# Remainders on GpSimd, accumulation moved ahead of a step's side work, and one operand made later, in a fused attention and mixture-of-experts kernel

## The chip, the cores and the metric

The kernel runs on one core of a Trainium2 chip. Times are device microseconds (us) of one execution. The kernel before was timed three times: 1437.53 us in the median, from 1435.39 to 1437.68. A further execution was taken with the hardware profiler; it lasted 1436.41 us, and the span of its instructions is 1434.6 us. The program's instructions are issued in order on five engines: TensorE (PE in the profile; its weight loads are PEld), VectorE (DVE), ScalarE (ACT), GpSimd (POOL) and the DMA-issuing queue of SyncE (SP).

## The reference

The attention part compresses 576 keys and values of each head to 32 memory slots with a softmax of phi, attends to these slots, and gives x; four experts, weighted by the given probabilities, follow.

```python
a = softmax(phi over seq)                       # 8 batches, 8 heads, 576 x 32
k_m = einsum('bhsm,bhsd->bhmd', a, k)           # 32 x 64 a head
v_m = einsum('bhsm,bhsd->bhmd', a, v)
attn = softmax(q @ k_m.T / sqrt(64))            # 576 x 32 a head
x = (attn @ v_m) as 4608 x 512
out = sum over e of p[:, e] * (relu(x @ w1[e]) @ w2[e])   # 512 -> 1024 -> 512, 4 experts
```

The inputs are fp32 and so is the result.

## The kernel before, in words

**Precision by two parts.** TensorE multiplies in fp32r, so an operand is kept as two tiles: its rounded part, made by a ScalarE copy, and its remainder, which is the source minus the rounded part. The helper `split` (lines 141 to 143) does that for weights: `nc.scalar.copy`, then `eng.tensor_sub` on the engine that it is given. A product is three matmuls (high by high, high by remainder, remainder by high).

**The main loop.** x is never formed. For each pair of batches k (4 pairs) and each expert e, v_m is multiplied into w1 once (the tiles `vw`), and the attention weights `AT` are multiplied by that. One pair and expert take 32 steps, so there are 512 steps in all; step s of an expert works on one of 8 blocks j of 128 hidden units, for one of four groups of rows. In a step, `first(s + 2)` makes six matmuls into a PSUM tile `p1` (lines 553 to 555), ScalarE takes the relu (line 565), and VectorE makes the remainder (line 567). `second(s)` multiplies the hidden block of two steps earlier by w2 into two PSUM tiles `p2`, three where the rows that straddle two batches (`hm`, `mid`) come along (lines 583 to 585). There are four `p2` tiles. After the eighth block, `accumulate` (lines 603 and 605, on VectorE) multiplies them by the probabilities, adds them to `acc` in SBUF and so frees them. The group with three tiles (steps 16 to 23 of an expert) starts with two free tiles; its third is one of the two that the group before has just filled, so the first matmul on `hm` at its first step waits for the first `accumulate` instruction.

**Side work.** A table `plan` assigns everything else to steps: loading and splitting the next expert's w1 and w2 (`units_w1`, `units_w2`, one split a step), the products v by w1 (`vw_mm`, line 453 to 455, into a PSUM tile `pv`) and their split (`vw_out`, lines 473 and 474: ScalarE, VectorE, ScalarE, VectorE for the two batches), or, for the pairs that go "by four" batches, `four` (lines 506 to 509) with the operand `vs` that holds v of four batches, written by `write_vs` (lines 367 to 370) from v and its rounded part `vh`. Attention of batches 2 to 7 is spread over steps too: the softmax of phi (lines 192 to 209), its transposes (`tpa`, `tpb`), the splits of k and v (`kv_split`, lines 266 and 267, two a step), of their last 64 rows (`tail_split`, lines 252 and 253), `kv_mm` (line 278) two steps after `kv_split`, `kv_pick` (lines 311 and 312) and the scores. The PSUM tiles `p1`, `pv`, `x`, `kvp`, `tpa`, `sc` and the like share one ring of four buffers (tag `pm`), so a new one waits until the one four allocations before it has been read.

**What sets the order.** The start of the program and everything from step 36 (`FREE`) on is issued in the order in which it is written. Between them, steps 0 to 35 are ordered by the scheduling layer. Within a step the code ran `run_plan(s)` (the side work), `accumulate()`, `first(s + 2)`, `second(s)`. Sources arrive through four staging buffers by DMAs that SyncE issues three sources ahead; a buffer is free again when both parts of both its splits have been made.

Of the kernel before, what the change touches and what calls it, by code (L numbers as in the profile page):

```python
# [91 lines left out]
def body(ctx: ExitStack, tc: tile.TileContext, qm, qt, kv, kvt, phi, prob, w1, w1d, w2, out):  # L92
# [60 lines left out]
                split_w1(raw, fh, 2 * g + i, nc.vector)  # L153
        return ("w1", e, fh, g), emit

    def split_w2(k, e, j, raw):
        t = wp.tile([P, 2, DM], F32R, name="w2", tag="w2", bufs=NJ + 1)
        split(t, raw[:, j % 2, :], nc.vector)
        w2t[k, e, j] = t

    def units_w1(e, fh, g):
        kept = []
        def load(raw):
            kept.append(raw)
            split_w1(raw, fh, 2 * g, nc.vector)
        return (("w1", e, fh, g), load), lambda: split_w1(kept[0], fh, 2 * g + 1, nc.vector)

    def unit_w2(k, e, j2):
        def emit(raw):
# [4 lines left out]
    def units_w2(k, e, j2):  # L174
        kept = []
        def load(raw):
            kept.append(raw)
            split_w2(k, e, 2 * j2, raw)
        return (("w2", e, j2), load), lambda: split_w2(k, e, 2 * j2 + 1, kept[0])


    st = {}
# [72 lines left out]
    def unit_tail(b):  # L255
        def emit(raw):
            for h in range(2):
                tail_split(b, raw, h, nc.gpsimd if b == 1 else nc.vector)
        return ("kvt", b), emit

    def kv_split(b, hp, raw, c2, eng):
# [39 lines left out]
    def kv_pick(b, g):  # L301
        if g == 0:
            st["v", b] = att.tile([P, NP, M], F32, name="v", tag="v", bufs=2)
        for w in range(2):
            for i in range(2):
                r, m = slice(64 * i, 64 * i + 64), slice(M * i, M * i + M)
                lo = slice(2 * M + M * i, 2 * M + M * i + M)
                a = slice(2 * g, 2 * g + 2)
                dst = st["v", b][r, a] if w else kT[b % 4][r, a, m]
                src = st["kvp", b, g][r, :, w]  # L310
                (nc.vector.tensor_copy if i else nc.scalar.copy)(dst, src[:, :, m])
                nc.vector.tensor_add(dst, dst, src[:, :, lo])

    def unit_kv(b, hp):
# [16 lines left out]
    def v_hi(b, gs=slice(0, 2)):  # L331

        if ("vh", b) not in st:
            st["vh", b] = att.tile([P, NP, M], F32R, name="vh", tag="vh")
        split = lambda t: t.rearrange("p (g a) m -> p g a m", g=2)
        v, vh = split(st["v", b]), split(st["vh", b])
        if gs is not None:
            nc.scalar.copy(vh[:, gs], v[:, gs])
        return v, vh
# [154 lines left out]

    def four_split(raw, i):
        w = wp.tile([P, 2, 512], F32R, name="w1", tag="w1", bufs=4)
        split(w, raw[:, i, :], nc.vector)
        return w

    def four(n, e, fh, h, w):  # L500
# [114 lines left out]
    def att_units(b):  # L615
        u = [lambda g=g: (phi_turn(b, g), phi_turn_out(b, g)) for g in range(2)]
        u += [lambda: (phi_turn_tail(b), phi_turn_tail_out(b)), unit_tail(b)]
        u += [unit_kv(b, hp) for hp in range(NP)]
        def write():
            v_hi(b)  # L620
            if b < 4:
                write_vt(b)
            write_vs(b)
        u += [write]
        u += [unit_scores(b, t0) for t0 in (0, 2, 4)]
        u += [lambda t0=t0: (transposes(b, t0), transposes_out(b, t0)) for t0 in (0, 2, 4)]
        return u
# [8 lines left out]
    rest += [lambda hp=hp: vw_unit(0, 0, 1, hp, (0,), ("pm", 4)) for hp in range(NP)]  # L636
    for s, u in zip(REST_0, rest):
        at(s, u)
    at(4, lambda: (v_hi(0), write_vs(0)))

    at(UNITS_1[0], lambda: phi_chain(1))
    for i, u in enumerate(att_units(1)):
# [6 lines left out]
    def attention(b, s, scores, turns):  # L649
# [11 lines left out]
        for hp in range(NP):  # L661
            def load(raw, hp=hp):
                for c2 in range(2):
                    kv_split(b, hp, raw, c2, nc.vector)
            def multiply(hp=hp):
                for c2 in range(2):
                    kv_mm(b, hp, c2)
# [177 lines left out]

    def steps(a, b):
        for s in range(a, b):
            run_plan(s)
            accumulate()
            first(s + AHEAD)  # L850
            second(s)

# [44 lines left out]
```

## Time and profile before

| | before |
|---|---|
| median of 3 runs | 1437.53 us |
| profiled execution, its span | 1436.41 us, 1434.6 us |
| TensorE matmuls busy | 1399.7 us, 7748 instructions |
| VectorE busy | 815.8 us, 1877 instructions |
| ScalarE busy | 562.7 us, 1496 instructions |
| GpSimd busy | 29.1 us, 31 instructions |
| mean granted TensorE clock | 0.996 |

Busy time of TensorE is the union of matmuls whose ends are modelled, so matmuls overlap in it; time in which it is not busy is time in which it had nothing that could start. In the rows of groups, a line of the kernel, an engine and an operation are followed by out<-in names with their shapes and the number of instructions, then busy time in us and the mean of one in ns, then the idle time just before them and what ended it. In the table by windows, each row gives a stretch (us from the span's start), its length, the busy time of each engine with the number of instructions that it had there, the granted clock as a fraction, the DMA share and GB/s. In the list of waits, a row gives the waiting group, the group waited for, the total in us, how often, and the longest. In the timeline, a row gives start and length in us, engine, line, operation; square brackets hold idle time before it and what ended that.

### The profile page before, as it was taken

To read this page: it belongs to the slowest core of one execution; us is meant where nothing else is said; L and a number is where in the kernel's file an instruction comes from. 1 tells how busy PE (TensorE), PEld (TensorE's weight loads), DVE (VectorE), ACT (ScalarE), POOL (GpSimd) and SP (SyncE) were. 2 spreads that over 40 slices of the span, in tenths; PEclk is the share of its full clock that TensorE was granted. 3 is DMA by queue.
4 is the path that set the end of the run, shared out by engine and by line. 5 is a ranking of instruction groups with operands and counts; after the bars stand their busy time and mean duration, and the time that the engine had idled before them with its cause. 6 is when DMAs were issued, how large, how long until landed. Compare 5 with 4: busy or idle time off the path is not lost.

```text
span 1434.6 us, 21439 instructions
## 1 busy us (share of the span) xinstructions
PE 1399.7 (98%) x7748; PEld 1217.1 (85%) x7748; DVE 815.8 (57%) x1877; ACT 562.7 (39%) x1496; POOL 29.1 (2%) x31
## 2 busy tenths in 40 slices
PE   8899999999999989999999999999999999999998
PEld 7788878888888868878888888888888888888887
DVE  7885666756656576675564556646553434242432
ACT  6655445533344453453343443534332222222221
POOL 4300000000000000000000000000000000000000
PEclk9999999999999999999999999999999999999999
DMA  6532322575233243233568677686751633332201
GB/s 218 191 106 88 106 62 94 195 253 164 78 99 110 68 123 100 63 119 108 147 230 264 216 265 210 230 241 211 251 158 45 184 74 103 74 103 74 59 30 37
DMA packets 62840, 199.13 MB, mean 139 GB/s; under 512 B 10384, under 2 KB 11536, under 8 KB 62736
## 3 DMA queue, kind: packets, MB, share of 16 engines
q1 hardware_dynamic: 62736, 197.77, 44.1%
q8 instruction: 62, 1.02, 0.3%
q14 instruction: 42, 0.34, 0.1%
HBM read 146.35 MB, written 51.38 MB: 138 GB/s over the span
## 4 chain that ended last, share of the span: by engine, by line
PE 88%; DVE 6%; ACT 3%; DMA 2%; issue 1%; ACTq 0%; DVEq 0%
PE p L585 17%; PE p L583 17%; PE p L584 17%; PE p L553 9%; PE p L555 9%; PE p L554 9%; PE pv L506 2%; PE sc L383 2%; PE x L278 2%; DVE vw L474 1%; DVE w L143 1%; ACT vw L473 1%; DMA vwd<-vst 1%; PE tp L433 1%; ACT w L142 1%
## 5 line engine op out<-in xcount | busy, mean ns | idle before, releaser
L567 DVE SCALAR_TENSOR_TENSOR h<-p,h 128x256 fp32r<-128x256 f32 x512 | 214.7, 420 | 334.8 <-ACT h L565 221.3
L585 PE MATMUL p<-w,h 128*128 128x512 f32 x1024 | 402.5, 393 | 1.0 <-DVE nm L195 1.0
L583 PE MATMUL p<-w,h 128*128 128x512 f32 x1024 | 401.6, 392 | 0.0
L584 PE MATMUL p<-w,h 128*128 128x512 f32 x1024 | 400.9, 392 | 0.0
L565 ACT ACTIVATE h<-p 128x256 fp32r<-128x256 f32 x512 | 196.6, 384 | 481.5 <-PE p L555 463.1
L553 PE MATMUL p<-AT,vw 128*128 128x256 f32 (+1 forms) x1024 | 308.7, 301 | 10.5 <-DVE vw L474 5.2
L554 PE MATMUL p<-AT,vw 128*128 128x256 f32 (+1 forms) x1024 | 302.5, 295 | 0.7 <-DVE AT L445 0.7
L555 PE MATMUL p<-AT,vw 128*128 128x256 f32 (+1 forms) x1024 | 303.1, 296 | 0.1
L585 PEld LDWEIGHTS p<-w,h 128*128 128x128 f32 x1024 | 192.1, 188 | 44.4 <-DVE nm L195 1.5
L553 PEld LDWEIGHTS p<-AT,vw 128*128 128x128 f32 x1024 | 193.3, 189 | 32.7 <-issue 5.8
L583 PEld LDWEIGHTS p<-w,h 128*128 128x128 f32 x1024 | 192.7, 188 | 22.4 <-ACT h L565 0.3
L584 PEld LDWEIGHTS p<-w,h 128*128 128x128 f32 x1024 | 192.4, 188 | 22.2
L554 PEld LDWEIGHTS p<-AT,vw 128*128 128x128 f32 x1024 | 193.3, 189 | 20.4 <-DVE AT L445 1.2
L555 PEld LDWEIGHTS p<-AT,vw 128*128 128x128 f32 x1024 | 193.0, 189 | 0.5 <-issue 0.2
L143 DVE TENSOR_TENSOR w<-stage,w 128x512 fp32r<-128x512 f32 x259 | 179.0, 693 | 11.2 <-ACT w L142 4.9
L142 ACT CAST w<-stage 128x512 fp32r<-128x512 f32 x262 | 161.0, 617 | 8.2 <-DMA stage<-in_w 6.0
L567 DVE SCALAR_TENSOR_TENSOR hm<-p,hm 128x64 fp32r<-128x64 f32 x256 | 55.6, 217 | 119.4 <-ACT h L565 119.1
L565 ACT ACTIVATE hm<-p 128x64 fp32r<-128x64 f32 x256 | 56.9, 222 | 159.1 <-PE p L555 159.1
L509 DVE TENSOR_TENSOR vst<-pv,vst 128x512 fp32r<-128x512 f32 x80 | 55.3, 691 | 95.5 <-ACT vst L508 95.5
L508 ACT CAST vst<-pv 128x512 fp32r<-128x512 f32 x80 | 47.0, 587 | 125.0 <-PE pv L506 125.0
L474 DVE TENSOR_TENSOR vw<-pv,vw 64x512 fp32r<-64x512 f32 x94 | 64.4, 687 | 25.6 <-ACT vw L473 24.5
L473 ACT CAST vw<-pv 64x512 fp32r<-64x512 f32 x94 | 54.3, 581 | 43.7 <-DVE vw L474 34.1
(96 smaller groups left out, 1121.2 us busy)
## 6 DMA issues: line engine op xcount, KB each, us to landing
stage<-in_w SPq DMA_DIRECT2D x92, 512.0 KB, 4.0
vwd<-vst SPq DMA_DIRECT2D x80, 512.0 KB, 3.3
vw<-vwd SPq DMA_DIRECT2D x320, 128.0 KB, 4.0
stage<-in_w1d SPq DMA_DIRECT2D x40, 512.0 KB, 4.3
stage<-in_kv SPq DMA_DIRECT2D x32, 512.0 KB, 4.0
stage<-in_qm SPq DMA_DIRECT2D x16, 512.0 KB, 4.5
out<-acc SPq DMA_DIRECT2D x32, 256.0 KB, 2.1
ph<-in_phi SPq DMA_DIRECT2D x16, 288.0 KB, 4.2
```

The costliest lines, as they stand in the source:

```text
L142: nc.scalar.copy(dst[:, 0, :], raw)
L143: eng.tensor_sub(dst[:, 1, :], raw, dst[:, 0, :].bitcast(F32))
L473: nc.scalar.copy(t[r, 0, :], ps[r])
L474: nc.vector.tensor_sub(t[r, 1, :], ps[r], t[r, 0, :].bitcast(F32))
L553: nc.tensor.matmul(ps, w[:, 0, f], at_t[:, g, 0, c], start=g == 0, stop=False)
L554: nc.tensor.matmul(ps, w[:, 0, f], at_t[:, g, 1, c], start=False, stop=False)
L555: nc.tensor.matmul(ps, w[:, 1, f], at_t[:, g, 0, c], start=False, stop=g == 1)
L565: nc.scalar.activation(t[:, 0, to], ps[:, at_], AF.Relu)
L567: nc.vector.scalar_tensor_tensor(t[:, 1, to], ps[:, at_], 0.0, t[:, 0, to].bitcast(F32), ALU.max, ALU.subtract)
L583: nc.tensor.matmul(po[t], x[:, 0, :], w[:, 0, :], start=j == 0, stop=False)
L584: nc.tensor.matmul(po[t], x[:, 0, :], w[:, 1, :], start=False, stop=False)
L585: nc.tensor.matmul(po[t], x[:, 1, :], w[:, 0, :], start=False, stop=j == NJ - 1)
```

## The change

Five things change. The remainder of w1, w2 (in `units_w1`, `units_w2` and `four_split`) and of k and v (in `kv_split` of batches 2 to 7 and in `tail_split`) goes from VectorE to GpSimd; the rounded part stays on ScalarE. The splits that steps 0 to 35 make by `unit_w1` and `unit_w2` stay on VectorE. In `kv_pick` of batches 1 to 7 the second of each pair of copies goes from VectorE to ScalarE. `accumulate()` stands ahead of `run_plan(s)` in a step. `write_vs` of batches 0 and 1 is done at steps 20 and 21 and no longer at step 4 and in batch 1's units, and `vh` has two buffers so that it can wait that long.

```diff
-    def split_w2(k, e, j, raw):
+    def split_w2(k, e, j, raw, eng=nc.vector):
...
-        split(t, raw[:, j % 2, :], nc.vector)
+        split(t, raw[:, j % 2, :], eng)
...
-            split_w1(raw, fh, 2 * g, nc.vector)
-        return (("w1", e, fh, g), load), lambda: split_w1(kept[0], fh, 2 * g + 1, nc.vector)
+            split_w1(raw, fh, 2 * g, nc.gpsimd)
+        return (("w1", e, fh, g), load), lambda: split_w1(kept[0], fh, 2 * g + 1, nc.gpsimd)
...
-            split_w2(k, e, 2 * j2, raw)
-        return (("w2", e, j2), load), lambda: split_w2(k, e, 2 * j2 + 1, kept[0])
+            split_w2(k, e, 2 * j2, raw, nc.gpsimd)
+        return (("w2", e, j2), load), lambda: split_w2(k, e, 2 * j2 + 1, kept[0], nc.gpsimd)
...
-                tail_split(b, raw, h, nc.gpsimd if b == 1 else nc.vector)
+                tail_split(b, raw, h, nc.gpsimd)
...
-                (nc.vector.tensor_copy if i else nc.scalar.copy)(dst, src[:, :, m])
+                (nc.vector.tensor_copy if i and b == 0 else nc.scalar.copy)(dst, src[:, :, m])
...
-            st["vh", b] = att.tile([P, NP, M], F32R, name="vh", tag="vh")
+            st["vh", b] = att.tile([P, NP, M], F32R, name="vh", tag="vh", bufs=2)
...
-        split(w, raw[:, i, :], nc.vector)
+        split(w, raw[:, i, :], nc.gpsimd)
...
-        def write():
-            v_hi(b)
-            if b < 4:
-                write_vt(b)
-            write_vs(b)
-        u += [write]
+        u += [lambda: write_vt(b)]
...
-    at(4, lambda: (v_hi(0), write_vs(0)))
+    for b in range(2):
+        at(20 + b, lambda b=b: (v_hi(b), write_vs(b)))
...
-                    kv_split(b, hp, raw, c2, nc.vector)
+                    kv_split(b, hp, raw, c2, nc.gpsimd)
...
-            run_plan(s)
             accumulate()
+            run_plan(s)
             first(s + AHEAD)
             second(s)
```

Counted over the program, 224 remainders of weights (line 143), 48 of k and v (line 267) and 12 of the last rows (line 253) leave VectorE for GpSimd, and 28 small copies (line 311) leave VectorE for ScalarE.

Around step 48, VectorE's rows before. `kT` and `v` are the sums of `kv_pick`, `vt` is batch 2's v as an operand (step 48's side work), `acc` the accumulation of the group that step 47 ended:

```order
L567 SCALAR_TENSOR_TENSOR hm<-p_2069,hm 128x64
L567 SCALAR_TENSOR_TENSOR h<-p_2069,h 128x256
L143 TENSOR_TENSOR w_2089<-stage,w_2089 128x512
L354 CAST vt_82<-vh 64x2x32
...
L207 RECIPROCAL zs<-zs 128x1
L208 TENSOR_SCALAR ph<-ph,zs 128x576
L209 COPY ph<-ph 128x64
L605 SCALAR_TENSOR_TENSOR acc<-p_1879,pt,acc 128x512
L605 SCALAR_TENSOR_TENSOR acc<-p_1883,pt,acc 128x512
L567 SCALAR_TENSOR_TENSOR hm<-p_2108,hm 128x64
```

and the same place of the change:

```order
L567 SCALAR_TENSOR_TENSOR hm<-p_2069,hm 128x64
L567 SCALAR_TENSOR_TENSOR h<-p_2069,h 128x256
L605 SCALAR_TENSOR_TENSOR acc<-p_1879,pt,acc 128x512
L605 SCALAR_TENSOR_TENSOR acc<-p_1883,pt,acc 128x512
L354 CAST vt_82<-vh 64x2x32
```

The two accumulations stand right behind step 49's remainder of the hidden block; thirteen instructions that stood ahead of them (a weight's remainder, eight on `vt`, four on phi) now follow or are gone.

Around steps 157 to 159, VectorE's rows before, where w2's remainder stands ahead of `vw_out` in each step:

```order
L567 SCALAR_TENSOR_TENSOR h<-p_5276,h 128x256
L143 TENSOR_TENSOR w_5292<-stage,w_5292 128x512
L474 TENSOR_TENSOR vw<-pv,vw 64x512 x2
L232 TENSOR_TENSOR a<-tpa,a 128x2x4x64
L567 SCALAR_TENSOR_TENSOR h<-p_5310,h 128x256
L143 TENSOR_TENSOR w_5328<-stage,w_5328 128x512
L474 TENSOR_TENSOR vw<-pv,vw 64x512 x2
L232 TENSOR_TENSOR a<-tpa,a 128x2x4x64
L253 TENSOR_TENSOR tl<-stage,tl 64x512 x2
```

and GpSimd's rows of the change for steps 157 to 160:

```order
L143 TENSOR_TENSOR w_5257<-stage,w_5257 128x512
L143 TENSOR_TENSOR w_5292<-stage,w_5292 128x512
L143 TENSOR_TENSOR w_5328<-stage,w_5328 128x512
L253 TENSOR_TENSOR tl<-stage,tl 64x512 x2
L143 TENSOR_TENSOR w_5372<-stage,w_5372 128x512
L267 TENSOR_TENSOR kvs<-stage,kvs 128x512 x2
```

On VectorE the rows of lines 143 and 253 are gone there, and `vw_out` follows the hidden block's remainder directly; on GpSimd nothing but these remainders stands in the queue.

More of the change, by code (lines that the diff above doesn't have):

```diff
@@ L847, in steps @@
         for s in range(a, b):
+            accumulate()
             run_plan(s)
-            accumulate()
             first(s + AHEAD)
```

## The prediction

> **What bounds the kernel now.** I read the page's busy shares first, then the table by windows, then the waits of TensorE, then the timeline at each long wait.
>
> ```profile
> PE 1399.7 (98%) x7748; PEld 1217.1 (85%) x7748; DVE 815.8 (57%) x1877; ACT 562.7 (39%) x1496; POOL 29.1 (2%) x31
> ```
>
> TensorE is the bound: 1399.7 of 1434.6 us. The change takes no matmul away, so all that it can win lies in the 34.9 us in which TensorE is not busy, and in what a lowered clock costs. Where these lie:
>
> ```profile
> 186.00:250.00 64.00, 58.77 (x316) 50.11 (x315) 43.44 (x103) 29.64 (x75) 0.00 (x0) 0.97 0.27 83
> ...
> 292.00:460.00 168.00, 168.00 (x955) 146.92 (x954) 101.64 (x225) 66.71 (x172) 0.00 (x0) 1.00 0.44 136
> ...
> 500.00:520.00 20.00, 14.07 (x73) 10.77 (x72) 15.80 (x36) 10.96 (x23) 0.00 (x0) 1.00 0.17 53
> ...
> 564.00:576.00 12.00, 9.78 (x47) 7.90 (x46) 11.22 (x36) 5.46 (x18) 0.00 (x0) 0.86 0.38 129
> ...
> 608.00:624.00 16.00, 12.96 (x72) 10.62 (x71) 11.37 (x20) 9.78 (x21) 0.00 (x0) 1.00 0.30 98
> ```
>
> From 292 to 460 nothing is idle. Four short stretches hold 5.23, 5.93, 2.22 and 3.04 us of idle TensorE, 16.4 us together, and in each VectorE has much work (15.80 of 20 us, 11.22 of 12). In two of them the granted clock is below 1. Whom TensorE waits for:
>
> ```profile
> PE p L583 <- DVE acc L605: 6.6, 5, 3.1
> PE p L553 <- DVE vw L474: 5.2, 5, 1.7
> ...
> PE p L553 <- ACT xs L289: 2.6, 2, 1.3
> ```
>
> So it waits for VectorE to free a `p2` tile by accumulating, or for VectorE (or ScalarE behind it) to free a buffer of the `pm` ring. VectorE is late there because its queue holds work that nobody waits for yet.
>
> **The change, part by part.** First what is moved costs:
>
> ```profile
> L267 POOL TENSOR_TENSOR kvs<-stage,kvs 128x512 fp32r<-128x512 f32 x10 | 13.2, 1333 | 14.9 <-ACT kvs L266 14.8
> L253 POOL TENSOR_TENSOR tl<-stage,tl 64x512 fp32r<-64x512 f32 x4 | 5.7, 1440 | 19.0 <-ACT tl L252 18.9
> L143 POOL TENSOR_TENSOR w<-stage,w 128x512 fp32r<-128x512 f32 x3 | 3.8, 1282 | 7.5 <-ACT w L142 7.5
> ...
> L143 DVE TENSOR_TENSOR w<-stage,w 128x512 fp32r<-128x512 f32 x259 | 179.0, 693 | 11.2 <-ACT w L142 4.9
> ```
>
> A remainder takes 693 ns on VectorE and 1282 on GpSimd. The 224 + 48 + 12 = 284 moved ones free VectorE of about 284 x 0.69 = 196 us and give GpSimd 224 x 1.28 + 48 x 1.33 + 12 x 1.44 = 368 us. GpSimd does nothing else, and a step takes over 2 us, so one remainder a step, and two or three in a few, fit. The Trainium skill (GPSIMD Engine Reference, Engine selection) speaks against this: it would keep elementwise work on VectorE, as about twice as fast. The rows here agree (1.85 times); by that rule the move would lose, if the path ran through GpSimd.
>
> *Step 48.* VectorE before, and the clock of its effect below:
>
> ```profile
> 190.18 0.68 DVE L143 TENSOR_TENSOR w<-stage,w 128x512 fp32r<-128x512 f32 x1
> 190.88 0.19 DVE L354 CAST vt<-vh 64x64 fp32r<-64x64 f32 x1
> ...
> 193.28 1.41 DVE L605 SCALAR_TENSOR_TENSOR acc<-p,pt,acc 128x512 f32<-128x512 f32 x2
> ```
>
> The accumulation starts 3.10 us behind the weight's remainder, at 193.28. In the new order it stands where L143 stood, and an earlier L143 of the step before is gone too: it starts at 190.2 less 0.6, plus some tenths for the `kv_pick` that now hands over between two engines each time. The longest wait of the list, 3.1 us (this one), goes but for about 0.3. What follows it runs slowly, as after the second such place, where the group behind step 175 is accumulated:
>
> ```profile
> 566.97 0.39 PE L584 MATMUL p<-w,h 128*128 128x512 f32 x1
> 567.20 0.40 PE L585 MATMUL p<-w,h 128*128 128x512 f32 x1
> 569.82 0.64 PE L583 MATMUL p<-w,hm 128*128 128x512 f32 x1 [2.22 <-DVE acc L605]
> 570.27 0.63 PE L584 MATMUL p<-w,hm 128*128 128x512 f32 x1
> ```
>
> Matmuls start 0.23 us apart before the wait and 0.45 after it, so three of them lose 0.66; with the next few I put the slow clock at 0.9 us (estimate). In the stretch from 500, whose granted clock is 1.00, no wait was over 1.73 us. The Trainium skill (TensorE: Matmul & The Clock Gate, HAM oscillation) names idle gaps above 3.4 us as what lowers the clock. Here 2.22 did; by its figure the 0.9 us would be no part of this wait's price. Step 48 is worth 3.1 - 0.3 + 0.9 = 3.7 us.
>
> *Step 176.* There the queue is late already before the accumulation's place:
>
> ```profile
> 568.43 0.68 DVE L143 TENSOR_TENSOR w<-stage,w 128x512 fp32r<-128x512 f32 x1
> 569.02 1.40 DVE L605 SCALAR_TENSOR_TENSOR acc<-p,pt,acc 128x512 f32<-128x512 f32 x2
> ```
>
> Only remainders that leave count, this one and one at step 174, 0.6 us each: 2.22 falls to about 1.1, which is under 1.73, so the 0.9 of slow clock goes as well. 2.0 us.
>
> *The other third tiles* (step 144 and four places in the `four` stages, of which this is step 80):
>
> ```profile
> 289.24 0.68 DVE L143 TENSOR_TENSOR w<-stage,w 128x512 fp32r<-128x512 f32 x1
> 289.83 1.40 DVE L605 SCALAR_TENSOR_TENSOR acc<-p,pt,acc 128x512 f32<-128x512 f32 x2
> ...
> 290.63 0.50 PE L583 MATMUL p<-w,hm 128*128 128x512 f32 x1 [0.42 <-DVE acc L605]
> ```
>
> 0.42 us each; `acc` now comes two instructions earlier (1.3 us), so all five go: 5 x 0.42, or 2.0 us. What it costs: VectorE's side work of such a step stands behind an `acc` that waits for the last matmul of `second`, and behind its 1.4 us (2.1 with three tiles). Queued there are `vst` and `vw` remainders and then the hidden block's; these are needed a step later, over 2 us off. I take nothing for it; bounds 0 and 0.7 us at each of some ten steps with dense side work.
>
> *Steps 155 to 159.* Each `vw_out` is a chain of four instructions on two engines:
>
> ```profile
> 510.25 0.68 DVE L143 TENSOR_TENSOR w<-stage,w 128x512 fp32r<-128x512 f32 x1
> 510.97 0.69 DVE L474 TENSOR_TENSOR vw<-pv,vw 64x512 fp32r<-64x512 f32 x1
> 512.31 0.68 DVE L474 TENSOR_TENSOR vw<-pv,vw 64x512 fp32r<-64x512 f32 x1 [0.65 <-ACT vw L473]
> ...
> 513.14 0.36 PE L553 MATMUL p<-AT,vw 128*128 128x256 f32 x1 [1.73 <-DVE vw L474]
> ```
>
> The wait at 513.14 ends with the second L474; L143 stands ahead of the first. Five steps lose one L143 each, 5 x 0.69 = 3.4 us; the 0.65 between the two L474 stays, and so does the chain's own length. Of 5.93 us 3.4 go.
>
> *Steps 188 to 191 and 58 to 62.* The same chain, but ScalarE is nearly full there (9.78 of 16 us, and the waits for `xs` end on it, which the change does not shorten). Of the 3.04 us at 608 to 624 I take off 1.2, two remainders less the handoffs; of the 2.1 us left at 186 to 250, 0.5. *Steps 0 to 35*: `write_vs` leaves a crowded place for steps 20 and 21; the scheduling layer reorders there, so -1.5 to +1.5 us, and I take 0.5 as gain. Copies of `kv_pick` on ScalarE add 28 x 0.2 us and handoffs, in steps where it has room: nothing.
>
> **Against this: GpSimd beside VectorE.**
>
> ```profile
> L208 DVE TENSOR_SCALAR ph<-ph,zs x16: 520/520/1558, 5.9 to 644.5; 128x576 f32<-128x576 f32 x16
> ```
>
> Minimum, median and maximum of 16: 1558 ns is from the start, with GpSimd busy, 1.04 us over the median. Operations that read and write SBUF alone seem to be held until a GpSimd one ends; for those with an operand in PSUM (L474, L567, L605) no row shows it. GpSimd will be busy for 368 us of about 1000, so each run of such operations is hit one time in three or so. Some five runs lie in the stretches above: 5 x 1.04 x 0.37 = 1.9 us on VectorE, half of it on the path: 1.0. Staging buffers come free up to 1.28 - 0.69 = 0.6 us later; DMAs are issued three sources ahead, so 0.5 us in all.
>
> **Sum.** 3.7 + 2.0 + 2.0 + 3.4 + 1.2 + 0.5 + 0.5 = 13.3 gained, 1.5 lost: 11.8. The profiled execution took 1436.4 us, so 1424.6; the median of the runs is 1.1 above it, which gives 1425.7, say 1425.5. VectorE's busy time should fall to about 815.8 - 196 - 6 = 614 and rise by holds to 620 to 635; GpSimd's should be 390 to 420.
>
> **Rivals.**
>
> *All of these waits go* (0.14). The handoffs turn out to have slack once VectorE is free: 16.4 + 2.0 + 2 x 0.9 = 20.2 us off, 1417.5. For it: the stretch from 292 to 460 has eight `vw_out` steps (115 to 128), without phi work, and no idle TensorE. Against: 0.65 us handoffs in every pair.
>
> *Only the accumulations are mended* (0.07). Then 3.7 + 2.0 + 2.0 less 1.5, 6.2 off: 1431. For it: the `xs` waits end on ScalarE.
>
> *VectorE is held by GpSimd* (0.10). Each of the five runs is hit in full, 5.2 us and not 1.0: 4.2 less, 1430. The Trainium skill (GPSIMD Engine Reference, Specifications) says that the two engines share SBUF interfaces, and that VectorE instructions with two SBUF inputs or in a two-port mode contend. The L208 row agrees.
>
> *The waits only change their name* (0.06): ScalarE's chain takes over at once and the clock stays: 1436 to 1438.
>
> *Slower: GpSimd is late with k and v* (0.06).
>
> ```profile
> PE x L278 <- POOL kvs L267: 0.3, 1, 0.3
> ```
>
> This wait exists already where GpSimd makes them. `kv_mm` comes two steps behind the ScalarE copies, 4.2 us at least (a step is six matmuls 0.23 us apart and six of half the columns). Two copies and two remainders in a row take about 0.6 + 2 x 1.33 = 3.3 us. It decides where ScalarE or GpSimd is over 0.9 us behind. At 0.5 us for each of 24 `kv_mm` of batches 2 to 7 the gain is gone; at one remainder each, 24 x 1.33 = 32 lost, 1437.5 - 11.8 + 32 = 1458. Against: GpSimd has an idle step between most of them.
>
> The remaining 0.57 is the forecast, 1425.5, itself good to 4 us. The range that leaves out about 2 in 10 is 1417.5 to 1433. Under 0.2% (2.9 us) is about what a measurement of this kernel cannot tell from no change. Faster by more: 0.57 + 0.14 + 0.07 + 0.10 = 0.88; within: 0.06; slower: 0.06.
>
> **What would show it.** `acc` gone from the list of TensorE's waits but for about one 1 us entry; TensorE idle at 500 to 520 down to some 2.5 us; granted clock 1.00 at both places; L143 on GpSimd at 1.28 to 1.4 us. I am wrong if waits for `kvs`, `w` or `tl` on GpSimd reach microseconds, if L208, L209, L369, L370 or L412 grow by a half in the mean, or if TensorE loses more in steps 0 to 35.

## The result, and the profile after

The changed kernel takes 1424.39 us (median; 1424.31 to 1424.42), the kernel before, on the same chip, 1436.46 (1435.09 to 1437.68). The ratio is 0.9916, with a 95% interval of 0.9899 to 0.9933: 0.84% faster. Its profiled execution lasted 1424.37 us with a span of 1422.6, against 1434.6 before. So 12.0 us went, where 11.8 had been forecast (1425.5, range 1417.5 to 1433). The total was right. Its parts were not, as the sections below show: one term has the wrong sign, another was four times too small, and with smaller misses they nearly cancel. Three of the experiments below had one execution each that took 1956 us or more at a granted clock of 0.30 to 0.65; medians and ratios are over the others.

The busy shares of its page:

```profile
PE 1396.9 (98%) x7748; PEld 1217.2 (86%) x7748; DVE 653.1 (46%) x1565; ACT 568.6 (40%) x1524; POOL 395.3 (28%) x315
```

The table by windows, for the stretches that answer to those shown of before:

```profile
184.00:246.00 62.00, 59.73 (x331) 50.90 (x330) 33.46 (x83) 32.40 (x82) 27.83 (x22) 1.00 0.29 94
...
287.00:455.00 168.00, 168.00 (x955) 147.13 (x954) 81.94 (x188) 66.33 (x173) 46.96 (x38) 1.00 0.44 138
...
494.00:511.00 17.00, 11.84 (x55) 8.96 (x55) 11.96 (x23) 9.03 (x18) 5.63 (x5) 0.90 0.20 63
...
511.00:600.00 89.00, 86.91 (x509) 76.10 (x508) 44.67 (x114) 40.25 (x112) 35.29 (x28) 1.00 0.33 103
...
600.00:615.00 15.00, 12.68 (x72) 10.36 (x71) 6.74 (x13) 9.91 (x24) 9.57 (x8) 1.00 0.34 107
```

TensorE's longest waits:

```profile
PE p L553 <- DVE vw L474: 3.1, 4, 1.4
PE x L278 <- DVE a L232: 2.7, 1, 2.7
PE p L553 <- DVE h L567: 2.4, 2, 2.3
PE p L553 <- ACT xs L289: 2.3, 2, 1.2
...
PE p L583 <- DVE acc L605: 2.0, 2, 1.5
```

In the stretch of step 48 (186 to 250 before, 184 to 246 now) TensorE's idle time fell from 5.23 us to 2.27, and the clock there is 1.00 now (0.97 before); the stretch around step 176 (inside 511 to 600) has 1.00 where it had 0.86. The waits for `acc` fell from 6.6 us to 2.0. But the stretch of steps 157 to 159 (494 to 511) still has 5.16 us of idle TensorE, after 5.93, and its clock is now 0.90 where it was 1.00. The longest wait for `h` was 1.3 us before; it is 2.3 now, and lies there.

Idle time alone misses the price of a slow clock, so I compare steps by the time from the end of the last `second` matmul of one step to that of another, worked out from the timelines. Steps that are not named differ by less than 0.1 us.

| steps | before | after | difference | forecast |
|---|---|---|---|---|
| start to the end of 36 | 159.98 | 157.78 | -2.20 | -0.5 |
| 48, 49 | 11.22 | 7.08 | -4.14 | -3.7 |
| 50 to 56 | 22.98 | 23.37 | +0.39 | 0 |
| 57 to 64 | 27.48 | 26.73 | -0.75 | -0.5 |
| third tiles at 80, 144, and in 261 to 340 (three) | 307.29 | 303.83 | -3.46 | -2.0 |
| 157 to 159 | 16.78 | 17.20 | +0.42 | -3.4 |
| 161 to 163 | 7.34 | 8.51 | +1.17 | 0 |
| 176, 177 | 11.25 | 8.88 | -2.37 | -2.0 |
| 188 to 191 | 16.51 | 15.77 | -0.74 | -1.2 |
| 208 to 260 | 141.19 | 140.92 | -0.27 | 0 |
| not placed: VectorE held, staging late | | | | +1.5 |

(The third tiles are counted by the stretches 80, 113 to 144, 261 to 299 and 300 to 340.)

VectorE's rows around step 48 now. The first columns are start and length:

```profile
186.80 1.22 DVE L209 COPY ph<-ph 128x64 f32<-128x64 f32 x1
188.03 0.23 DVE L567 SCALAR_TENSOR_TENSOR hm<-p,hm 128x64 fp32r<-128x64 f32 x1
188.17 0.41 DVE L567 SCALAR_TENSOR_TENSOR h<-p,h 128x256 fp32r<-128x256 f32 x1
188.50 1.40 DVE L605 SCALAR_TENSOR_TENSOR acc<-p,pt,acc 128x512 f32<-128x512 f32 x2
```

The accumulation stands right behind `h` and starts 0.33 us after it, where it had stood 3.10 us behind a weight's remainder. The first row is new: a copy of 64 columns that takes 1.22 us, with a median of 0.20. It is the first sign of what went wrong at step 157.

### The profile page after: what moved, and what is told of

It is laid out like the page before. It is cut to its first block, busy times and chain, and to the rows that moved or that the text cites. A ratio compares the mean times of both kernels' runs of the same rounds, so it can differ in the third digit from the quotient of the medians.

```text
span 1422.6 us, 21651 instructions
## 1 busy us (share of the span) xinstructions
PE 1396.9 (98%) x7748; PEld 1217.2 (86%) x7748; DVE 653.1 (46%) x1565; ACT 568.6 (40%) x1524; POOL 395.3 (28%) x315
## 4 chain that ended last, share of the span: by engine, by line
PE 91%; DVE 4%; ACT 3%; DMA 1%; issue 1%; POOL 0%; SPq 0%; ACTq 0%; DVEq 0%
PE p L585 18%; PE p L584 17%; PE p L583 17%; PE p L553 9%; PE p L555 9%; PE p L554 9%; PE pv L506 3%; PE x L278 2%; PE sc L383 2%; DVE vw L474 1%; ACT vw L473 1%; ACT w L142 1%; PE tp L433 1%; PE pv L453 1%; DMA stage<-in_w 1%
## 5 line engine op out<-in xcount | busy, mean ns | idle before, releaser
L143 POOL TENSOR_TENSOR w<-stage,w 128x512 fp32r<-128x512 f32 x227 | 293.2, 1294 | 734.0 <-ACT w L142 710.4
L267 POOL TENSOR_TENSOR kvs<-stage,kvs 128x512 fp32r<-128x512 f32 x58 | 75.0, 1314 | 98.9 <-ACT kvs L266 98.0
```

Source lines behind the costliest of these rows:

```text
L143: eng.tensor_sub(dst[:, 1, :], raw, dst[:, 0, :].bitcast(F32))
L267: eng.tensor_sub(t[:, 1], src, t[:, 0].bitcast(F32))
```

## The experiments

**One part alone.** Three kernels each make one part of the change in the kernel before. The first has only the order:

```diff
-            run_plan(s)
             accumulate()
+            run_plan(s)
```

> The kernel before, with only the accumulation moved ahead of a step's side work. Theory (each part mends its own places): at step 48 the first accumulation no longer stands behind a weight's remainder and 2.4 us of side work, so the 3.07 us wait and the slow clock behind it go, -3.8; the five short waits for a third p2 tile go, -2.9 (0.58 us each from start to start of matmuls); at step 176 only one remainder moves behind it, -0.7. Steps 155 to 159 and 188 to 191 stay as they were. Sum -7.4, about 1429 us. Rival (the accumulation is only early enough once the remainders have left VectorE): step 48 keeps over 1.5 us, the sum is -3 or less, 1433 us or more.

1429.68 us, ratio 0.9957 (0.9942 to 0.9971), span 1427.4: in sum as the theory has it. One moved line brings 7.2 of the 12.0 us between the profiled executions (6.4 of 12.1 between the medians). Steps 48 and 49 take 6.53 us (-4.69, more than with the whole change), 176 and 177 9.03 (-2.22, where -0.7 was expected), step 80 3.39 (-0.70, all that the whole change brings there). But it takes something back too: 50 to 56 are 1.59 longer, 161 to 163 1.08, 193 to 207 0.68. Its waits:

```profile
PE p L553 <- DVE vw L474: 5.9, 7, 1.7
...
PE p L583 <- DVE acc L605: 1.6, 1, 1.6
```

The waits for `acc` are down from 6.6 us to 1.6, and those for `vw` are up from 5.2 in five places to 5.9 in seven: side work that stands behind an `acc` now comes later.

The second has only the remainders of w1, w2, k, v and the last rows on GpSimd (`split(..., nc.gpsimd)` in `units_w1`, `units_w2`, `four_split`, `kv_split`, `tail_split`):

> The kernel before, with only the remainders of w1, w2, k and v given to GpSimd. Theory: step 48 gains 1.3 (two remainders ahead of the accumulation), step 176 1.2 to 2.1, the five short waits 2 to 2.9, steps 188 to 191 0.7; steps 155 to 159 gain nothing, because what VectorE saves there it loses again while it is held by GpSimd, as in the changed kernel (+0.4), and the k and v of step 160 come late (+1.2). Sum -3 to -5, about 1432 us. Rival (the remainders are the whole gain, and the accumulation's place only follows): -9 or more, 1427 us. Rival (GpSimd beside VectorE costs more than it gives without the earlier accumulation): 1436 us or more.

1432.01 us, ratio 0.9969 (0.9958 to 0.9979), span 1429.2: in sum as expected. 176 and 177 (8.88) and step 80 (3.47) gain nearly as much as by the order alone, so the two parts in good part cure the same waits and their gains do not add. Steps 48 and 49, which were expected to gain 1.3 us, get longer (12.15, +0.93), and the waits show why:

```profile
PE p L583 <- DVE acc L605: 5.5, 2, 4.0
...
PE p L553 <- DVE h L567: 2.3, 1, 2.3
```

The wait for `acc` at step 48 was 3.1 us and is 4.0, though VectorE has less to do. Two of the instructions ahead of that `acc` are stretched, each beside a remainder on GpSimd; their medians are 0.20 and 0.22:

```profile
189.13 1.17 DVE L209 COPY ph<-ph 128x64 f32<-128x64 f32 x1
...
190.99 1.29 DVE L355 TENSOR_TENSOR vt<-v,vh 64x64 fp32r<-64x64 f32 x1
```

The third has only `write_vs` of batches 0 and 1 later:

```diff
-    at(4, lambda: (v_hi(0), write_vs(0)))
+    for b in range(2):
+        at(20 + b, lambda b=b: (v_hi(b), write_vs(b)))
```

> The kernel before, with only the operand of 4 batches of batches 0 and 1 moved to steps 20 and 21. Theory (the 1.8 us wait for the transposes of phi at 55.9 us, behind write_vs of batch 0 with its 1.19 us copy, and the order of steps 0 to 35 that follows from it, are what the changed kernel won in its first 36 steps): from the first matmul of line 553 to the end of step 36 is 3 to 4 us shorter than the 130.8 us of before, 1433 us. Rival (the changed kernel's first 36 steps are shorter through the copies of kv_pick on ScalarE and the tails and k, v of batch 2 on GpSimd): within 1 us of before, 1436 us.

1433.99 us, ratio 0.9985 (0.9976 to 0.9994), span 1433.1; from the first matmul on `vw` (line 553) to the end of step 36 it takes 127.81 us and not 130.76. The 2.95 us are just under the 3 to 4 expected; 1.6 of them are given back because that first matmul came later, at 30.83 and not 29.22 (below). In all twelve profiles of this document that stretch takes 129.77 to 130.76 us in the three without this part, and 126.35 to 128.15 in the nine with it. In the kernel before, the casts of `write_vs` stood ahead of phi's normalization on VectorE, one of them stretched, and TensorE waited for phi. VectorE's row of that, in the timeline of before:

```profile
52.78 1.19 DVE L369 CAST vs<-vh 64x64 fp32r<-64x64 f32 x1
```

and TensorE's:

```profile
55.90 0.66 PE L223 MATMUL tpa<-ident,ph 128*128 128x128 f32 x4 [1.80 <-DVE ph L208]
```

In this kernel, the list of waits has of that:

```profile
PE tpa L223 <- DVE ph L208: 0.4, 1, 0.4
```

**The failed steps, 157 to 159.** In the timeline of the changed kernel, VectorE has three long rows there (start, length, instruction):

```profile
491.61 1.34 DVE L370 TENSOR_TENSOR vs<-v,vh 64x64 fp32r<-64x64 f32 x1
...
498.02 1.18 DVE L208 TENSOR_SCALAR ph<-ph,zs 128x576 f32<-128x576 f32 x1
499.23 1.14 DVE L209 COPY ph<-ph 128x64 f32<-128x64 f32 x1
500.29 0.41 DVE L567 SCALAR_TENSOR_TENSOR h<-p,h 128x256 fp32r<-128x256 f32 x1
```

GpSimd's rows at the same time (the second stands for two instructions):

```profile
491.58 1.30 POOL L143 TENSOR_TENSOR w<-stage,w 128x512 fp32r<-128x512 f32 x1 [16.76 <-ACT w L142]
...
497.61 2.71 POOL L143 TENSOR_TENSOR w<-stage,w 128x512 fp32r<-128x512 f32 x2 [4.74 <-ACT w L142]
```

and TensorE, which waits behind them:

```profile
500.75 0.39 PE L553 MATMUL p<-AT,vw 128*128 128x256 f32 x1 [2.25 <-DVE h L567]
```

L370 takes 1.34 us where its median is 0.22, L208 1.18 for 0.52, L209 1.14 for 0.20. L370 and L209 end within 0.1 us of the end of a GpSimd instruction that was running beside them (492.95 and 492.88; 500.37 and 500.32). These are holds, 2.7 us in all, and `h` stands behind two of them. One rival is that the queue is merely long. So in the next kernel just these three remainders go back to VectorE, which gives it 3 x 0.69 us more to do, and takes GpSimd out of its way:

```diff
-    def units_w1(e, fh, g):
+    def units_w1(e, fh, g, eng=nc.gpsimd):
...
-                for i, u in enumerate(units_w2(nk, ne, j2)):
+                for i, u in enumerate(units_w2(nk, ne, j2, nc.vector if s == PAIR and j2 == 0 else nc.gpsimd)):
...
-                    for i, u in enumerate(units_w1(ne, fh, g)):
+                    for i, u in enumerate(units_w1(ne, fh, g, nc.vector if s == PAIR and fh and g else nc.gpsimd)):
```

> The changed kernel, with three remainders (w1 at steps 155 and 156, the first of w2 at step 157) back on VectorE, so that GpSimd is idle while VectorE runs write_vs of batch 4 and the two norms of phi. Theory (VectorE was held by GpSimd there: L370 1.34, L208 1.18, L209 1.14 us instead of 0.22, 0.52, 0.20): these rows go back to their medians, 2.7 us less, against 3 x 0.69 = 2.1 us more on VectorE; steps 155 to 159 end 0.6 us earlier or more, by up to 1.5 where the wait gets too short to lower the clock: 1422.9 to 1423.8 us against 1424.4. Rival (VectorE simply has too much to do there, and the held rows are not on the path): the 2.1 us come on top, 1426 us or more.

1422.72 us, ratio 0.9907 (0.9887 to 0.9927), 1.67 below the changed kernel, though with more on VectorE: a little under the hold theory's range, and the load rival (1426 or more) falls. The same rows are at their medians again:

```profile
490.57 0.69 DVE L143 TENSOR_TENSOR w<-stage,w 128x512 fp32r<-128x512 f32 x1
491.29 0.22 DVE L370 TENSOR_TENSOR vs<-v,vh 64x64 fp32r<-64x64 f32 x1
...
497.18 0.52 DVE L208 TENSOR_SCALAR ph<-ph,zs 128x576 f32<-128x576 f32 x1
497.73 0.20 DVE L209 COPY ph<-ph 128x64 f32<-128x64 f32 x1
```

The wait for `h` is 1.3 us there, and 157 to 159 take 16.40 us, 0.80 less than in the changed kernel (1.29 less than in its second profile, below). Of the 1.67 us only this half belongs to the theory: 1.04 lie before the end of step 36, which the edit does not touch and where executions differ as much (below). By the steps alone, then, giving three remainders back gains 0.8 to 1.3 us here, and the load would have cost, not gained.

**Small copies on ScalarE.** The second copies of `kv_pick` go back to VectorE:

```diff
-                (nc.vector.tensor_copy if i and b == 0 else nc.scalar.copy)(dst, src[:, :, m])
+                (nc.vector.tensor_copy if i else nc.scalar.copy)(dst, src[:, :, m])
```

> The changed kernel, with the second copy of each pair in kv_pick of batches 1 to 7 back on VectorE. Theory (four copies on ScalarE, each waiting for VectorE's sum of the one before, take as long as two and two): within 0.7 us of the changed kernel from the first matmul of line 553 to the end, some tenths shorter at steps 175 to 177. Rival (taking the copies off VectorE is a real part of the gain): 1 us or more longer, at steps 49 and 177 above all.

1424.52 us, ratio 0.9925 (0.9908 to 0.9941): no difference that can be told. 57 to 64 gain 0.53 by it; 157 to 159 lose 0.79 (17.99), or 0.30 against the changed kernel's second profile (below). The places that the rival named do not get longer by it: 48 and 49 take 6.99 us (7.08 in the changed kernel), 176 and 177 8.93 (8.88). From the first matmul on `vw` to the end it is 1.65 us longer than in the changed kernel's first profile and 0.53 longer than in its second, so the 0.7 expected as a bound is neither kept nor broken.

**The phi work moved away.** If the holds are one part of the trouble at 157 to 159, a larger one may be that phi work of batch 5 (L208, L209, the transposes and L232) stands in the very steps in which each `vw_out` chain must be finished within a step. The next kernel starts batch 5's attention seven steps later, and makes `write_vs` of batch 4 nine steps later:

```diff
-    5: (PAIR + 22, (PAIR + 76, PAIR + 80, PAIR + 84), (PAIR + 112, PAIR + 113, PAIR + 114)),
+    5: (PAIR + 29, (PAIR + 76, PAIR + 80, PAIR + 84), (PAIR + 112, PAIR + 113, PAIR + 114)),
...
-        at(s + 27, lambda: write_vs(b))
+        at(s + (36 if b == 4 else 27), lambda: write_vs(b))
```

> The changed kernel, with batch 5's attention work started at step 157 and no longer at 150, and write_vs of batch 4 at step 164 and no longer 155: the norms of phi, the transposes and write_vs leave the steps that make vw. Theory (in steps 157 to 159 VectorE, held or not, has more work than TensorE's step is long, and the pm ring passes it on): the three steps take 2.8 us each as vw steps without phi do, 8.4 together against 17.2; of the 8.8 us 1.6 are transposes that come later, so -7, about 1417 us. Rival (the chain ScalarE, VectorE, ScalarE, VectorE of vw itself sets these steps): -3 or less, 1421 us or more. Rival (the work is missed at its new place): 1424 us or more, with new waits at steps 164 to 183.

1413.41 us, ratio 0.985 (0.9836 to 0.9865): 11.0 below the changed kernel, and more than the 7 expected. 157 to 159 take 8.34 us, 2.8 each, and not 17.20; that is 8.86 us. It also takes 2.02 off 161 to 163 and 1.72 off 176 and 177, where less side work is left to be late, and adds 1.05 and 1.50 where the work has gone (164 to 175, 178 to 187). I had not counted these four. From step 37 on it is 10.05 us; the rest lies in the first steps. (Which of the two moves does how much was not tried.)

The next one moves batches 6 and 7 as well, out of steps 188 to 191 and out of the place that batch 5 now takes:

```diff
-    6: (PAIR + 44, (2 * PAIR + 24, 2 * PAIR + 28, 2 * PAIR + 32), (2 * PAIR + 29, 2 * PAIR + 33, 2 * PAIR + 37)),
-    7: (PAIR + 66, (2 * PAIR + 98, 2 * PAIR + 102, 2 * PAIR + 106), (2 * PAIR + 112, 2 * PAIR + 113, 2 * PAIR + 114)),
+    6: (PAIR + 62, (2 * PAIR + 24, 2 * PAIR + 28, 2 * PAIR + 32), (2 * PAIR + 29, 2 * PAIR + 33, 2 * PAIR + 37)),
+    7: (PAIR + 76, (2 * PAIR + 98, 2 * PAIR + 102, 2 * PAIR + 106), (2 * PAIR + 112, 2 * PAIR + 113, 2 * PAIR + 114)),
```

> As the one before, and batches 6 and 7 start at steps 190 and 204 and no longer at 172 and 194: no k and v work, softmax of phi or kv_pick stands in the vw steps 187 to 192 or ahead of the accumulation of step 176. Theory: beside the 7 us, the wait at step 176 goes (-1.7) and steps 188 to 191 lose theirs (-2): about 1413.5 us. Rival (steps 188 to 191 are ScalarE's own chain, and 176 stays behind the soft work of batch 4): as the one before, 1416 to 1417 us. Rival (the later batches come too late for the operand of 4 batches at step 232): waits of several us there.

1410.01 us (1409.5 to 1410.75), ratio 0.9825 (0.9809 to 0.9842). It beats both kernels: 14.4 us below the changed one (13.1 from step 37 on), more than the change itself brought, and 3.5 below what was expected. 188 to 191 take 11.13 us and not 15.77, and 178 to 187 30.47 and not 33.65 as in the kernel before this; 208 to 260, where batch 6's and 7's work now lies, take 146.07 and not 140.92, since matmuls of attention are moved there with it. Steps 157 to 177 and 188 to 191 by windows:

```profile
484.00:500.00 16.00, 16.00 (x87) 13.74 (x86) 8.57 (x17) 10.20 (x23) 5.73 (x5) 1.00 0.28 78
500.00:590.00 90.00, 90.00 (x520) 78.55 (x519) 51.80 (x126) 42.12 (x116) 31.50 (x26) 1.00 0.27 87
590.00:604.00 14.00, 14.00 (x80) 12.21 (x79) 10.25 (x21) 9.95 (x22) 7.57 (x6) 1.00 0.45 155
```

TensorE is not idle in any of them, and the clock is 1.00, with VectorE about as busy in the whole (653.2 us) as in the changed kernel (653.1). In these steps not how much VectorE has to do, but what stands ahead of a chain that must be short decides.

**How far a profile repeats.** The first 36 steps differ by microseconds between kernels that do the same there, so the changed kernel was profiled a second time, unaltered.

> The changed kernel once more, beside the others. Theory (the first 30 us vary from run to run with the first loads; from the first matmul of line 553 on, every step takes the same time again): from there to the end 1391.6 us to 0.2 us, and the span differs from 1422.6 by what the first 30 us differ. Rival (the steps vary too): differences of over 0.5 us in the stretches between the steps.

1424.13 us, ratio 0.9926 (0.991 to 0.9942), span 1422.5. From step 37 on all steps repeat to hundredths of a microsecond, but for step 157 (+0.46, in the place of the holds). The first matmul on `vw` came at 29.84 and not 30.98, and from there to the end of 36 it took 127.47 and not 126.80: the start gives 1.1 and the next steps take 0.7 of it back. So the 1391.6 us expected from there to the end came out as 1392.7: the steps repeat only from 37 on, and not all of them. Over twelve profiles the first one lay between 29.2 and 31.0.

**What GpSimd is worth.** The changed kernel with every moved remainder back on VectorE, that is order, copies and `write_vs` alone (`nc.vector` again in the five helpers):

> The changed kernel, with the remainders of w1, w2, k and v back on VectorE; the earlier accumulation, the later operand of 4 batches and kv_pick stay changed. Theory (the accumulation and the operand carry the gain; GpSimd's part is what steps 50 to 64 and 190 give, less what it costs at 157): from step 36 on as with the accumulation alone, 2.5 us longer than the changed kernel; the first 36 steps within 1 us of it; about 1426.5 us. Rival (the remainders on GpSimd are the main part): 1430 us or more.

1426.65 us, ratio 0.9934 (0.9912 to 0.9957), as expected. The 284 moved instructions, the bulk of the change, are worth 2.3 us in the medians (1.1 in the two profiled executions: 3.0 from step 37 on, less 1.9 before that). Step by step: 50 to 64 take 52.34 us with VectorE and 50.10 with GpSimd, 193 to 207 39.39 and 38.51, 188 to 191 16.50 and 15.77; against that 48 and 49 take 6.52 and 7.08, 157 to 159 16.76 and 17.20, and the start up to step 36 155.88 and 157.78. Its longest waits for the chains to `first`:

```profile
PE p L553 <- DVE vw L474: 4.9, 6, 1.5
PE p L553 <- DVE h L567: 2.6, 2, 1.4
```

And the best kernel with the remainders on VectorE, which asks whether GpSimd is needed once the phi work is gone:

> The version with batches 5, 6 and 7 started later, with the remainders of w1, w2, k and v back on VectorE. Theory (once the phi work is out of the vw steps, VectorE has room for the remainders there; only steps 50 to 64, where batch 3 is still among them, miss GpSimd, by 2.2 us): 1412 to 1413.5 us against 1410.4. Rival (GpSimd is what makes the room): 1416 us or more, with waits for vw at steps 157 to 160 and 187 to 192.

1414.6 us, ratio 0.985 (0.9831 to 0.987), span 1412.1: 4.6 above the kernel that it is made from (4.3 from step 37 on). It lies between the two expectations. No wait comes back at 157 to 159 (8.34 us), so those steps do not need GpSimd; it is lost in steps that lie elsewhere, most at 50 to 64 (52.37 us, 50.09 with GpSimd) and 161 to 163 (8.12, 6.49). So GpSimd is worth more in that kernel, and most of what makes the difference lies at 161 to 163, where the remainders on VectorE now cost 1.63, and not at the place of the holds.

## Why the prediction was right and wrong

**Step 48: right, slightly undersized.** It had 3.7 us for the wait and the slow clock, and measured is 4.14. Both causes are seen: the wait for `acc` is 0.49 (0.3 was forecast, the handoffs) and the clock is 1.00. The wait fell by 2.58 us, from 3.07; that leaves 1.56 for the clock, which was put at 0.9.

```profile
189.30 0.50 PE L583 MATMUL p<-w,hm 128*128 128x512 f32 x1 [0.49 <-DVE acc L605]
```

The order alone gives 4.69; the 0.55 between lies beside the held L209 row shown above (the order with VectorE's remainders, 6.52, has all of it). The remainders that leave, counted as part of it, made nothing better here: with them alone the wait is 4.0.

**Step 176: right in size, only half right in its reason.** 2.0 forecast, 2.37 measured, the clock is back at 1.00 and a wait is left:

```profile
562.61 0.50 PE L583 MATMUL p<-w,hm 128*128 128x512 f32 x1 [1.49 <-DVE acc L605]
```

1.1 was forecast for it. So the wait fell by 0.73 us and not 1.1, and 1.64 are left for the clock and not 0.9: the sum is right by two misses. I said that only the remainders that leave count. They do suffice (8.88 us for both steps), but so does the order (9.03) without any of them leaving.

**The other third tiles: a mis-sized term.** 5 x 0.42 was forecast (2.1, taken as 2.0), measured are 0.70, 0.62 and three times about 0.71, 3.46 in all. Step 80 takes 3.39 us now, 4.09 before. The 0.42 is an idle time between a modelled end and a start; the step was longer by more. The step-to-step time would have been the right row.

**"Accumulation ahead costs nothing": wrong at the value taken.** 0 was taken of 0 to 0.7 at each of some ten steps; the cost lies inside these bounds. By the kernel with the order alone it costs 1.59 at 50 to 56, 1.08 at 161 to 163 and 0.68 at 193 to 207, 3.4 together. In the changed kernel GpSimd takes most of the first and all of the last back; 161 to 163 stay 1.17 longer. There the rows behind step 160's accumulation in the timeline of the changed kernel are, on VectorE:

```profile
512.06 1.40 DVE L603 TENSOR_SCALAR acc<-p,pt 128x512 f32<-128x512 f32 x2
513.49 0.69 DVE L474 TENSOR_TENSOR vw<-pv,vw 64x512 fp32r<-64x512 f32 x1
```

on ScalarE:

```profile
514.22 0.58 ACT L473 CAST vw<-pv 64x512 fp32r<-64x512 f32 x1 [1.42 <-DVE vw L474]
```

and on TensorE:

```profile
518.25 0.62 PE L278 MATMUL x<-kvs,a 128*128 128x256 f32 x3 [0.48 <-POOL kvs L267]
```

`vw`'s remainder waits for the accumulation, ScalarE's second copy for it (1.42 us), the copies of k and v behind that on ScalarE for both, GpSimd's remainder for them, and `kv_mm` for that. This is the place that the slower rival named (GpSimd late with k and v); it cost 0.5 us at one place in the waits, not a remainder at each of 24. GpSimd is not its main cause: the same steps take 8.42 with the order alone (7.34 before), 8.40 with all of the change but GpSimd, and 7.84 with the remainders on GpSimd alone.

**Steps 155 to 159: the step that failed.** It said that five steps lose one L143 each, 5 x 0.69 = 3.4 us. They got 0.42 longer. Two things were wrong in it. First, L143 was not what the chain waited for. With all remainders on VectorE these three steps take 16.78 (before), 16.78 (order alone) and 16.76 us (no remainder moved); with them on GpSimd 17.20 and 17.74 (remainders alone). The most that came from L143 leaving is 0.4, in the kernel with three of them back and the others on GpSimd (16.40); without phi work the steps take 8.3 with the remainders on either engine. The instruction that stood directly ahead of the chain was taken as its cause, because it was the one that the change removes. Second, GpSimd held VectorE there, the rival that had 0.10. I spread it evenly (1.9 us on VectorE, half on the path). At this place it came to 2.7 us in three rows, behind which TensorE waited 2.25 us. The sign that the prediction had named for it came: the means of L209 and L370 grew by over a half (224 to 347 ns, 220 to 356). The lowered clock there, 0.90 over 17 us, is no proof of it: in the kernel with all of the change but GpSimd the clock over these steps was 0.90 too, in the one with the order alone 1.00, and in both they took 16.8 us. The rival as a whole did not win (1430), since its five runs were not all hit: 48 and 157 were, and the other holds lie in steps that take no longer than without GpSimd.

**Steps 188 to 191 and 58 to 62** were 0.74 and 0.75 for 1.2 and 0.5. Of the ScalarE limit it is right that the waits for `xs` stay (2.6 us before, 2.3 now).

**Steps 0 to 35: a mis-sized term.** 0.5 was taken of -1.5 to +1.5; it is 2.20 up to step 36, and 3.96 from the first matmul on `vw`. The wait of 1.80 us for phi at 55.90 was in the trace of before, and the working left out who stood ahead of it: `write_vs`, the very thing that the change moves.

**VectorE's busy time** was forecast at 620 to 635 us and is 653.1. The kernel with all remainders on VectorE has:

```profile
PE 1396.3 (98%) x7748; PEld 1216.8 (85%) x7748; DVE 807.0 (57%) x1849; ACT 568.3 (40%) x1524; POOL 29.8 (2%) x31
```

807.0 - 653.1 = 153.9 for 284 instructions; with the 14.1 us of holds (below) added it is 168.0, or 0.59 each and not 0.69. The means of the rows overlap their neighbours: before, L143 at 568.43 lasts 0.68, and the next starts at 569.02. GpSimd's 395.3 us (390 to 420) and its L143 were right:

```profile
L143 POOL TENSOR_TENSOR w<-stage,w 128x512 fp32r<-128x512 f32 x227 | 293.2, 1294 | 734.0 <-ACT w L142 710.4
```

So the 11.8 us came out by luck of sums. 155 to 159 were worse by 3.8, 161 to 163 by 1.2, 188 to 191 and 50 to 56 by 0.9 together; the start, the third tiles, step 48 and the rest were better by 1.7, 1.5, 0.4 and 0.9, and the unplaced loss of 1.5 was not a further one, since the holds lie in the steps above.

## What to carry to other kernels

Where a late engine is to be relieved, first try the order: putting the one instruction that frees a buffer ahead of side work brought 6.4 of 12.1 us (medians) with one line, while 284 instructions moved to an idle engine brought 2.3. Take as the cause of a wait not the instruction right ahead of it that can be moved, but each one in its chain that can be taken away, and price it from the step-to-step time; moving phi work and what hangs on it by 7 to 18 steps was worth 13 us. And where GpSimd works beside VectorE, place its instructions away from steps in which a short chain runs over VectorE's SBUF work.

## What was unexpected of the hardware

**Holds.** From 100 us on, 17 VectorE instructions of the changed kernel are over 0.25 us above the median of their line, 14.1 us in all and 1.13 at most. In the kernel before, in the one with the order alone and in the one with all remainders on VectorE there is none. Each of the 17 was running when a GpSimd remainder ended, and 15 of them ended 0.02 to 0.08 us after it; the other two, of lines 208 and 412, whose instructions take longest (0.52 and 0.69), 0.32 and 0.54 after it. So they seem to have stood until GpSimd was done. One line's instructions, minimum/median/maximum in ns, of the kernel before:

```profile
L370 DVE TENSOR_TENSOR vs<-v,vh x32: 218/221/224, 35.6 to 706.9; 64x64 fp32r<-64x64 f32 x32
```

and of the changed one:

```profile
L370 DVE TENSOR_TENSOR vs<-v,vh x32: 218/222/1349, 37.3 to 697.6; 64x64 fp32r<-64x64 f32 x32
```

Held were lines 208, 209, 354, 370, 410 and 412, all of which read and write SBUF alone; never 474, 567, 603 and 605, which read PSUM; the prediction had one row for the former and none for the latter. Which of the two starts first matters. In the changed kernel every instruction of these six lines that started while a remainder was running, and would have ended before it, was held; the one of line 208 and the three of 412 that had started 0.43 to 0.45 us ahead of a remainder took their usual time. SBUF alone is not enough: in the changed kernel and the best one, four reductions (lines 192 and 409, SBUF alone) started while a remainder was running that outlasted them by 0.45 to 0.51 us, and took their usual time. The second execution of the same kernel holds the same 17 (14.1 us), and the best kernel 20 (15.7 us): it is faster all the same, since many fall where nobody waits, six of them in the stretches from 484 to 604 in which TensorE is never idle. The Trainium skill (GPSIMD Engine Reference, Specifications) names VectorE instructions with two SBUF inputs or in a two-port mode as those that contend. The rows agree for 370 and 412, which have two SBUF inputs; for the copies and the scaling, which have one, it would be the mode, and no row here shows that. So the L208 row that the prediction called agreeing shows that the two engines contend, and not that its condition is met.

**The clock.** A wait of 2.22 us went with a granted clock of 0.86 over 12 us (step 176 before), and one of 2.25, with another of 1.19 about three microseconds ahead, with 0.90 over 17 (step 157 after). The stretches that lost their long waits are at 1.00. In the kernel with three remainders back, the longest waits of the stretch were 1.38 us, and the clock was as low:

```profile
493.00:509.00 16.00, 11.76 (x54) 8.84 (x53) 11.17 (x22) 8.87 (x18) 2.77 (x3) 0.89 0.20 67
```

Before, the same steps had waits up to 1.73 us at 1.00. So one wait's length does not decide it.

The record shows what goes with it, when it is asked in shorter stretches. In each of the twelve traces the clock changes only at instants that lie whole multiples of 3.41 us apart, and it is either 1.00 or 0.50; the 0.86, 0.90 and 0.89 are one such period at half clock, averaged over 12, 17 and 16 us. Three periods in a row of the kernel with the remainders alone on GpSimd (the first busy time is TensorE's, the third number from the end the clock):

```profile
189.60:193.00 3.40, 1.54 (x8) 0.96 (x6) 3.33 (x10) 1.29 (x5) 1.94 (x2) 1.00 0.24 96
193.00:196.40 3.40, 1.25 (x8) 1.07 (x9) 3.25 (x11) 0.00 (x0) 0.00 (x0) 1.00 0.46 154
196.40:199.80 3.40, 3.40 (x13) 3.01 (x12) 2.19 (x9) 0.98 (x3) 0.00 (x0) 0.50 0.00 0
```

and of the changed kernel:

```profile
495.00:498.40 3.40, 1.87 (x9) 0.90 (x7) 2.60 (x7) 1.97 (x5) 0.79 (x1) 1.00 0.00 0
498.40:501.80 3.40, 1.15 (x9) 1.01 (x8) 2.86 (x4) 0.87 (x2) 1.92 (x2) 1.00 0.50 149
501.80:505.20 3.40, 3.40 (x9) 2.52 (x8) 2.21 (x4) 2.59 (x6) 1.28 (x1) 0.50 0.03 13
```

From 20 us on to the last step, some 4900 periods in the twelve traces, a period at full clock was followed by half clock eleven times, and TensorE had been busy for 14 to 42% of each of those eleven; no other at full clock was busy for less than 45%. (Once, with the small copies back on VectorE, the clock stayed at half for a second period.) So it seems to go by the busy share of a period, and not by one wait. The periods fall at other places of the program in each execution, so the same waits can lie in one or be split between two. A period at half clock costs at most half of it, 1.7 us, beside the 1.56 and 1.64 found at steps 48 and 176. This is read from the traces of one kernel; no run here was made to test it. The Trainium skill (TensorE: Matmul & The Clock Gate, HAM oscillation) names idle gaps over 3.4 us as what to avoid. No wait in these stretches was as long as that (the longest was 3.07 us); the measurement decides.

**The start.** The same program reached its first matmul on `vw` at 30.98 us in one execution and at 29.84 in another, while the 475 steps from 37 on repeated to hundredths but for one. A difference below 2 us in the first 36 steps is not to be read from one profile; whether the remainders on GpSimd cost something there (155.88 us without, 157.78 and 157.31 with) stays open.
